# Score matmuls of a decode attention kernel rebuilt as column-tiled units of four octets, with a bf16 score stash and DVE transposes

## The chip, the cores and the metric

The kernel runs on one core of one Trainium2 chip. The metric is the device time of one execution in microseconds (us); the median of several executions is quoted. Engines are named as in the profile: PE is TensorE, DVE is VectorE, ACT is ScalarE, POOL is GpSimd, SP is the engine whose queue issues the loads. PEclk is the clock that the throttle grants to PE, as a share of full speed. PSUM is the on-chip memory into which the kernel lets PE write its results, SBUF the one that holds everything else on the chip. P·V is the product of the attention probabilities and the values. In the tile names, ktp holds K transposes in PSUM, sps scores and ops P·V; arena_k holds the loaded keys and, after the eviction, the transposed ones; arena_v holds the values.

## The reference

One decode step of an adaLN transformer block, one token, bf16. The attention reads a key and a value cache of 65,536 tokens for 8 heads, each shared by 4 query heads: 128 MB of keys and 128 MB of values. Everything else is small.

```python
mod = (silu(c) @ w_mod).reshape(...)                 # six modulation vectors
h = layernorm(x) * (1 + ca) + sa
# attention: Hq = 32, Hkv = 8, Sk = 65536, Dh = 128
q = (h @ wq) ...
scores = einsum('bhqd,bhkd->bhqk', q, k) * Dh ** -0.5   # k, v repeated 4 times
p = softmax(scores)
o = einsum('bhqk,bhkd->bhqd', p, v)
x = x + ga * (o ... @ wo)
h = layernorm(x) * (1 + cb) + sb
return x + gb * ((silu(h @ w_gate) * (h @ w_up)) @ w_down)
```

## The kernel before

Keys and values arrive in 2 MB chunks of 64 token tiles (a tile is 128 tokens), four chunk buffers each. A block of 8 tiles is called an *octet*; a head has 64 octets, a chunk 8. The main loop runs over octets. In step `s` it emits the transposition of octet `s+3` (PE) and its eviction to SBUF (DVE, or ACT for every fourth octet), then the scores of octet `s` (PE). The P·V product of an octet follows 72 octets behind its scores, two octets at a time. A small scheduler adds semaphore waits from declared reads and writes. It never reorders: each engine receives its instructions in the order of emission.

```python
def T_op(o):                     # 4 transposes of 128x128 f32 (pairs of bf16) into one of 3 PSUM banks
    ...
def evac_engine(o):
    if o % 4 == 3 and not in_exp_burst(o): return "act"
    return "dve"

def S_op(o):                     # scores: K is the stationary operand, the queries (M64) stream
    ...
    for pi_ in range(4):
        for par in range(2):
            insts.append(e.matmul(sps[:, sbank, REP*tl : REP*tl + 8*2*REP], lhsT=pair[:, :, par],
                                  rhs=M64[:, g, par, :, :], start=(par == 0), stop=(par == 1)))

def bank_ops(o):                 # once per 8 octets, on DVE: maximum, and a copy to SBUF (f32)
    op("dve", f"bmax{bl}", ...);  op("dve", f"bcopy{bl}", ...)

def head_softmax_ops(g):         # once per head: 8 exps on ACT write P_sb, [token, tile, query head]
    ...
def PVU_op(u):                   # two octets of P*V: 4 column-tiled matmuls
    ...
    for j in range(4):
        lhsT = P_sb[gp][:, tq:tq + 4, :].rearrange("p t h -> p (t h)")
        insts.append(e.matmul(ops_[32*j:32*j + 16, g % 2, 0:512], lhsT=lhsT, rhs=vnat[b][...],
                              start=first, stop=last, tile_position=(0, 32 * j)))
    op("pe", f"PVU{u}", emit, reads=[("vnat", b)] + [("P", gp, pi, h) ...], writes=[("ops", g % 2)])

for s in range(NKO + LV):        # NKO = 512 octets, LV = 72
    o = s + DT                   # DT = 3
    if o < NKO:
        T_op(o); pump_dma(); evac_op(o)
    if s < NKO:
        S_op(s)
        if s % OBL == OBL - 1: bank_ops(s)
        if s % OPH == OPH - 1: pending_heads[s + BC_OFF] = head_of(s)
    if s in pending_heads: head_softmax_ops(pending_heads.pop(s))
    vo = s - LV
    if 0 <= vo < NKO and vo % 2 == 1:
        PVU_op(vo // 2); pump_dma()
```

## Time and profile before

| | before |
|---|---|
| time, median of 16 runs | 696.16 us (695.25 to 698.64) |
| DMA while K and V both stream | 426 GB/s |
| PE / DVE / ACT busy | 79% / 48% / 24% |
| first P·V, last K transposes, end (trace) | 89.6, 624, 694 us |

From the page: the span, the busy us of each engine (share of the span), the rows of the 40 time slices of 17 us for the granted clock and for DMA (each digit in tenths), the GB/s of each slice, and the row of the main load queue (packets, MB, share):

```profile
span 694.0 us, 16865 instructions
...
PE 547.0 (79%) x7781; PEld 451.6 (65%) x7781; DVE 333.5 (48%) x594; ACT 166.9 (24%) x253; POOL 8.8 (1%) x33
...
PEclk9999999998999999999999989999999999996555
DMA  8999999999999999999999999999999999999996
GB/s 332 428 373 371 413 429 426 427 426 426 426 424 429 425 426 426 426 429 426 425 427 428 424 426 427 426 426 426 427 426 426 425 429 424 427 400 395 427 349 239
...
q1 hardware_dynamic: 26472, 285.48, 98.4%
```

DMA is at 9 in almost every slice and moves about 426 GB/s. 285 MB at that rate is 670 us. Clearly below the full rate are the first slice, slices 3 to 5 (only keys are consumed there) and four of the last five. The chain that ended last, by engine and then by line:

```profile
DMA 70%; PE 24%; SPq 4%; DVE 2%; issue 0%; POOL 0%; ACTq 0%; DVEq 0%
DMA arena_k<-in_A_k_cache_dram 39%; DMA arena_v<-in_A_v_cache_dram 24%; PE ktp L449 14%; PE sps L492 6%; SPq L285 4%; DMA xT_bf<-in_A_x_dram 3%; PE ops L559 3%; DMA arena_k<-in_B_w_down_dram 3%; PE misc L574 1%; DVE arena_k L475 1%; PE misc L419 1%; DVE X_sb L568 0%; DVE pm L504 0%; PE misc L675 0%; DVE S_sb L511 0%
```

It is mostly loads of keys and values (SPq is the queue of SP; "issue" is time without a wait that the profile shows). The costliest groups (line, engine, operation, count | busy us, mean ns of one | idle before and who ended it):

```profile
L449 PE MATMUL ktp<-identf,arena_k 128*128 128x128 f32 x2048 | 351.1, 297 | 63.1 <-DMA arena_k<-in_A_k_cache_dram 63.1
L475 DVE COPY arena_k<-ktp 128x512 f32<-128x512 f32 x398 | 274.8, 691 | 258.6 <-PE ktp L449 256.8
...
L492 PE MATMUL sps<-M,arena_k 128*128 128x64 bf16 x4096 | 213.3, 197 | 0.0
...
L559 PE MATMUL ops<-arena_v,P_sb 128*16 128x512 bf16 x1024 | 106.8, 430 | 31.8 <-DMA arena_v<-in_A_v_cache_dram 31.8
```

And a piece of the timeline in the middle (start us, length us, engine, line; lines of other engines left out). It shows P·V, transposes, scores, transposes, scores, P·V following each other on PE without idle time in brackets, that is, without a wait:

```profile
326.26 0.39 PE L559 MATMUL ops<-arena_v,P_sb 128*16 128x512 bf16 x4
...
326.58 0.66 PE L449 MATMUL ktp<-identf,arena_k 128*128 128x128 f32 x4
...
327.08 0.40 PE L492 MATMUL sps<-M,arena_k 128*128 128x64 bf16 x8
...
327.31 0.63 PE L449 MATMUL ktp<-identf,arena_k 128*128 128x128 f32 x4
...
327.78 0.40 PE L492 MATMUL sps<-M,arena_k 128*128 128x64 bf16 x8
...
328.11 0.39 PE L559 MATMUL ops<-arena_v,P_sb 128*16 128x512 bf16 x4
```

### The profile page before, as it was taken

How to read it: one execution, taken by the hardware profiler on the slowest of the kernel's cores; microseconds unless marked ns; L12 is line 12 of the kernel's file. 1: busy time of each engine (PE TensorE's matmuls, PEld its weight loads, DVE VectorE, ACT ScalarE, POOL GpSimd, SP SyncE). 2: the span in 40 equal slices, each digit the busy share in tenths (PEclk: the TensorE clock that was granted, in tenths of full speed). 3: DMA queues.
4: the chain of work that ended last, by engine and by line, in shares of the span. 5: the costliest groups of instructions: out<-in, count | busy, mean ns of one | idle time of the engine just before them, and what ended most of it. 6: DMA issues, size and time to landing. Idle time of an engine off the chain costs nothing.

```text
span 694.0 us, 16865 instructions
## 1 busy us (share of the span) xinstructions
PE 547.0 (79%) x7781; PEld 451.6 (65%) x7781; DVE 333.5 (48%) x594; ACT 166.9 (24%) x253; POOL 8.8 (1%) x33
## 2 busy tenths in 40 slices
PE   1399998888878798887788898878878798785345
PEld 1399987677766686766676686667666676672024
DVE  0178875454545554555454545536544554451001
ACT  0033442232222412123212411214121321223000
POOL 2000000000000000000000000000000000000000
PEclk9999999998999999999999989999999999996555
DMA  8999999999999999999999999999999999999996
GB/s 332 428 373 371 413 429 426 427 426 426 426 424 429 425 426 426 426 429 426 425 427 428 424 426 427 426 426 426 427 426 426 425 429 424 427 400 395 427 349 239
DMA packets 27598, 286.56 MB, mean 413 GB/s; under 512 B 3208, under 2 KB 9096, under 8 KB 10632
## 3 DMA queue, kind: packets, MB, share of 16 engines
q1 hardware_dynamic: 26472, 285.48, 98.4%
q8 instruction: 61, 1.00, 0.6%
q10 hardware_dynamic: 1056, 0.00, 0.1%
q14 instruction: 9, 0.07, 0.0%
HBM read 285.48 MB, written 0.00 MB: 411 GB/s over the span
## 4 chain that ended last, share of the span: by engine, by line
DMA 70%; PE 24%; SPq 4%; DVE 2%; issue 0%; POOL 0%; ACTq 0%; DVEq 0%
DMA arena_k<-in_A_k_cache_dram 39%; DMA arena_v<-in_A_v_cache_dram 24%; PE ktp L449 14%; PE sps L492 6%; SPq L285 4%; DMA xT_bf<-in_A_x_dram 3%; PE ops L559 3%; DMA arena_k<-in_B_w_down_dram 3%; PE misc L574 1%; DVE arena_k L475 1%; PE misc L419 1%; DVE X_sb L568 0%; DVE pm L504 0%; PE misc L675 0%; DVE S_sb L511 0%
## 5 line engine op out<-in xcount | busy, mean ns | idle before, releaser
L449 PE MATMUL ktp<-identf,arena_k 128*128 128x128 f32 x2048 | 351.1, 297 | 63.1 <-DMA arena_k<-in_A_k_cache_dram 63.1
L475 DVE COPY arena_k<-ktp 128x512 f32<-128x512 f32 x398 | 274.8, 691 | 258.6 <-PE ktp L449 256.8
L449 PEld LDWEIGHTS ktp<-identf,arena_k 128*128 128x128 f32 x2048 | 231.1, 148 | 120.2 <-issue 78.6
L477 ACT ACTIVATE arena_k<-ktp 128x1024 bf16<-128x1024 bf16 x114 | 116.7, 1024 | 441.4 <-PE ktp L449 441.4
L492 PE MATMUL sps<-M,arena_k 128*128 128x64 bf16 x4096 | 213.3, 197 | 0.0
L492 PEld LDWEIGHTS sps<-M,arena_k 128*128 128x128 bf16 x4096 | 200.4, 101 | 8.4 <-issue 0.2
L559 PE MATMUL ops<-arena_v,P_sb 128*16 128x512 bf16 x1024 | 106.8, 430 | 31.8 <-DMA arena_v<-in_A_v_cache_dram 31.8
L559 PEld LDWEIGHTS ops<-arena_v,P_sb 128*16 128x16 bf16 x1024 | 24.4, 89 | 56.8 <-DMA arena_v<-in_A_v_cache_dram 41.4
L526 ACT ACTIVATE P_sb<-S_sb,negm 128x64 bf16<-128x64 f32 (+1 forms) x64 | 47.1, 858 | 0.3
L504 DVE TENSOR_REDUCE pm<-sps 128x4 f32<-128x256 f32 x64 | 26.6, 416 | 2.0 <-PE sps L492 2.0
L511 DVE COPY S_sb<-sps 128x256 f32<-128x256 f32 x64 | 26.5, 414 | 0.0
L568 DVE COPY X_sb<-ops 128x512 f32<-128x512 f32 x8 | 5.5, 682 | 36.9 <-PE ops L559 36.9
L574 PE MATMUL misc<-sel,X_sb 128*128 128x4 f32 x64 | 10.1, 281 | 10.9 <-DVE X_sb L568 10.9
L574 PEld LDWEIGHTS misc<-sel,X_sb 128*128 128x128 f32 x64 | 9.6, 229 | 13.9 <-issue 7.2
L526 ACT ACTIVATION_READ_ACCUMULATOR P_sb<-S_sb,negm 128x1 f32 x64 | 14.2, 222 | 0.0
L379 PE MATMUL misc<-sT,arena_v 128*128 128x1 bf16 x96 | 2.7, 165 | 14.2 <-DVE sT L371 14.2
L661 ACT ACTIVATE g_e<-g_c 128x14 f32<-128x14 f32 x1 | 0.2, 214 | 54.9 <-DVE g_c L659 54.9
L379 PEld LDWEIGHTS misc<-sT,arena_v 128*128 128x128 bf16 x96 | 2.6, 104 | 14.2 <-issue 14.2
L509 POOL CROSS_LANE_REDUCE rmax<-pmax 128x4 f32<-128x4 f32 x8 | 3.9, 484 | 594.4 <-PE sps L492 384.0
L636 PE MATMUL misc<-attnT,arena_k 128*128 128x1 bf16 x128 | 3.6, 165 | 6.0 <-DMA arena_k<-in_A_wo_dram 6.0
L392 PE MATMUL misc<-xT,mmat 128*128 128x4 f32 x2 | 0.6, 350 | 8.8 <-DVE modT L383 8.8
L636 PEld LDWEIGHTS misc<-attnT,arena_k 128*128 128x128 bf16 x128 | 3.5, 104 | 6.2 <-DMA arena_k<-in_A_wo_dram 6.2
(85 smaller groups left out, 47.9 us busy)
## 6 DMA issues: line engine op xcount, KB each, us to landing
arena_k<-in_A_k_cache_dram SPq DMA_DIRECT2D x64, 2048.0 KB, 31.2
arena_v<-in_A_v_cache_dram SPq DMA_DIRECT2D x64, 2048.0 KB, 30.6
arena_v<-in_A_wq_dram SPq DMA_DIRECT2D x1, 4096.0 KB, 22.2
arena_k<-in_A_wo_dram SPq DMA_DIRECT2D x1, 4096.0 KB, 28.8
arena_v<-in_w_mod_dram SPq DMA_DIRECT2D x1, 3072.0 KB, 11.3
arena_k<-in_B_w_gate_dram SPq DMA_DIRECT2D x1, 1792.0 KB, 32.9
arena_k<-in_B_w_up_dram SPq DMA_DIRECT2D x1, 1792.0 KB, 14.6
arena_k<-in_B_w_down_dram SPq DMA_DIRECT2D x1, 1792.0 KB, 17.9
```

The costliest lines, as they stand in the source:

```text
L285: return [e.dma_start(out_ap, in_ap)]
L419: insts.append(e.matmul(misc[:, 64 + hd:64 + hd + 1], lhsT=wq_sb[:, kt, hd * P:(hd + 1) * P], rhs=hT[:, kt:kt + 1], start=(kt == 0), stop= ...
L449: insts.append(e.transpose(ktp[:, bank, pi_ * P:(pi_ + 1) * P], knat32[b][:, j * 4 + pi_, :], identf[:, :]))
L475: emit = lambda e: [e.tensor_copy(ring32[r], ktp[:, bank, :])]
L477: emit = lambda e: [e.activation(out=ring[r], in_=ktp[:, bank, :].bitcast(BF16), func=ACT.Copy)]
L492: insts.append(e.matmul(sps[:, sbank, REP * tl:REP * tl + 8 * 2 * REP], lhsT=pair[:, :, par], rhs=M64[:, g, par, :, :], start=(par == 0), ...
L504: op("dve", f"bmax{bl}", lambda e: [e.tensor_reduce(out=pm4[:, :, k], in_=hview, axis=AX.X, op=ALU.max)], reads=[("sps", sbank)], writes=[ ...
L511: op("dve", f"bcopy{bl}", lambda e: [e.tensor_copy(S_sb[gp][:, :, k * BLT:(k + 1) * BLT], hview)], reads=[("sps", sbank)], writes=[("S", g ...
L526: return [e.activation(out=P_sb[gp][:, t0:t1, h], in_=S_sb[gp][:, h, t0:t1], func=ACT.Exp, bias=negm[gp][:, h:h + 1], scale=SCALE, accum_o ...
L559: insts.append(e.matmul(ops_[32 * j:32 * j + 16, g % 2, 0:512], lhsT=lhsT, rhs=vnat[b][:, tl0 + 4 * j:tl0 + 4 * j + 4, :], start=first, st ...
L574: insts.append(e.matmul(misc[:, 8:8 + REP], lhsT=X_sb[:, tau * P:(tau + 1) * P], rhs=sel[:, tau, :], start=(tau == 0), stop=(tau == 3)))
L636: insts.append(e.matmul(misc[:, 96 + jb:96 + jb + 1], lhsT=wo_sb[:, kt, jb * P:(jb + 1) * P], rhs=attnT[:, kt:kt + 1], start=(kt == 0), st ...
```

## The change

Intent: PE loads 4,096 score weights of 128x128 for little work. The change swaps the operands: the queries, 8 columns, are stationary in four column tiles of the array, and the keys stream 512 wide. A *unit* of four octets then needs 8 matmuls instead of 32. The scores land with the query heads on partitions, 32 tokens wide per block. So the softmax has one exp over bf16 for all heads at once (copied out of PSUM by ACT into a stash), and the probabilities are brought back to tokens on partitions by a DVE transpose of 32x32 blocks and a compaction, just before each P·V group.

```diff
+        def SU_op(u):                                   # replaces S_op and bank_ops, once per 4 octets
+                for par in range(2):
+                    for a in range(4):
+                        insts.append(e.matmul(sps[32 * a:32 * a + 2 * REP, sbank, 0:512], lhsT=M8[:, g, par, :],
+                                              rhs=R4[:, :, 32 * a:32 * a + 32, par],
+                                              start=(par == 0), stop=(par == 1), tile_position=(0, 32 * a)))
+            op("dve", f"smax{u}", lambda e: [e.tensor_reduce(out=pmu[...], in_=sps[:, sbank, :], axis=AX.X, op=ALU.max)], ...)
+            op("act", f"scopy{u}", lambda e: [e.activation(out=S_st[gp][...], in_=sps[:, sbank, :], func=ACT.Copy)], ...)
 ...
         def PVU_op(u):
+            op("dve", f"ptr{u}", lambda e: [e.transpose(out=PTraw[wb][:, :], in_=S_st[gp][:, wh * 256:(wh + 1) * 256])], ...)
+            op("dve", f"pcp{u}", lambda e: [e.tensor_copy(PT[gp][...], PTraw[wb][...][:, :, 0:2 * REP])], ...)
-                    lhsT = P_sb[gp][:, tq:tq + 4, :].rearrange("p t h -> p (t h)")
+                    lhsT = PT[gp][:, tq * REP:(tq + 4) * REP]
-               reads=[("vnat", b)] + [("P", gp, pi, h) for pi in pis for h in range(REP)],
+            op("pe", f"PVU{u}", emit, reads=[("vnat", b), ("PT", gp, wh)], writes=[("ops", g % 2)])
 ...
-                S_op(s)
-                if s % OBL == OBL - 1:
-                    bank_ops(s)
+                if s % SU == SU - 1:
+                    SU_op(s // SU)
```

Cut: buffers, masks that pick a head's rows for the maximum and the sums, the exps.

More of the change, by code (lines that the diff above doesn't have):

```diff
@@ L144, in bass_adaLN_cond__gqa_block_cached__swiglu_ffn__decode_kernel @@
     CPH = TPH // TPC
-    BLT = min(64, TPH)
-    WN = 16
-    assert REP * BLT + 8 * 2 * REP <= 512
-    OBL = BLT // 8
-    NBL = TPH // BLT
+    SU = 4
+    assert OPH % SU == 0
+    UPH4 = OPH // SU
     NKO = HKV * OPH
@@ L155, in bass_adaLN_cond__gqa_block_cached__swiglu_ffn__decode_kernel @@
     RT = 8
+    assert RT % SU == 0
     NB = 3
@@ L162, in bass_adaLN_cond__gqa_block_cached__swiglu_ffn__decode_kernel @@
     EPS = 1e-5
-    if TPH > TPC:
-        PIECES = [(0, TPC), (TPC, TPH)]
+    U0 = max(1, OPC // SU)
+    if UPH4 > U0:
+        PIECES = [(0, U0), (U0, UPH4)]
     else:
-        PIECES = [(0, TPH)]
+        PIECES = [(0, UPH4)]
     NPIECE = len(PIECES)
@@ L205, in bass_adaLN_cond__gqa_block_cached__swiglu_ffn__decode_kernel @@
         wq_sb = arena_v[:, 2 * CH_ELEMS: 2 * CH_ELEMS + wq_elems].rearrange("p (kt n) -> p kt n", n=HQD)
-        S_sb = [sb(f"S_sb{i}", [P, REP, TPH], FP32) for i in range(2)]
-        P_sb = [sb(f"P_sb{i}", [P, TPH, REP], BF16) for i in range(2)]
+        S_st = [sb(f"S_st{i}", [P, UPH4 * 512], BF16) for i in range(2)]
+        PT = [sb(f"PT{i}", [P, TPH * REP], BF16) for i in range(2)]
+        PTraw = [sb(f"PTraw{i}", [P, 256], BF16) for i in range(2)]
         ident = sb("ident", [P, P], BF16)
@@ L214, in bass_adaLN_cond__gqa_block_cached__swiglu_ffn__decode_kernel @@
         M8 = sb("M8", [P, HKV, 2, 2 * REP], BF16)
-        M64 = sb("M64", [P, HKV, 2, 8, 2 * REP], BF16)
         mmat = sb("mmat", [P, P], FP32)
@@ L234, in bass_adaLN_cond__gqa_block_cached__swiglu_ffn__decode_kernel @@
         qT = sb("qT", [P, HQ], BF16)
-        pm4 = sb("pm4", [P, REP, NBL], FP32)
-        pmax = sb("pmax", [P, REP], FP32)
+        pmu = sb("pmu", [P, UPH4], FP32)
+        pmax_p = sb("pmax_p", [P, 1], FP32)
+        pm4 = sb("pm4", [P, REP], FP32)
+        onehot = sb("onehot", [P, REP], FP32)
+        maskneg = sb("maskneg", [P, REP], FP32)
+        negt = sb("negt", [P, REP], FP32)
         rmax = sb("rmax", [1, REP], FP32)
-        negm = [sb(f"negm{i}", [P, REP], FP32) for i in range(2)]
-        lpart = sb("lpart", [P, HQ, NPIECE], FP32)
-        lsum = sb("lsum", [P, HQ], FP32)
+        negm_p = [sb(f"negm_p{i}", [P, 1], FP32) for i in range(2)]
+        lpart = sb("lpart", [P, HKV, NPIECE], FP32)
+        lsum_all = sb("lsum_all", [P, HKV], FP32)
+        lsum = sb("lsum", [P, HKV, REP], FP32)
         rl = sb("rl", [P, HQ], FP32)
@@ L319, in bass_adaLN_cond__gqa_block_cached__swiglu_ffn__decode_kernel @@
             op("dve", f"opsz{i}", lambda e, i=i: [e.memset(ops_[:, i, :], 0.0)], writes=[("ops", i)])
+            op("dve", f"spsz{i}", lambda e, i=i: [e.memset(sps[:, i, :], 0.0)], writes=[("sps", i)])
+        op("pool", "oh0", lambda e: [e.memset(onehot[:, :], 0.0)], writes=[("onehot",)])
+        for a in range(4):
+            for tau in range(2):
+                op("pool", f"oh{a}{tau}", lambda e, a=a, tau=tau: [e.affine_select(out=onehot[:, :], in_=onehot[:, :], pattern=[[-1, REP]],
+                                                                                 compare_op=ALU.not_equal, fill=1.0,
+                                                                                 base=-(32 * a + 4 * tau), channel_multiplier=1)],
+                   reads=[("onehot",)], writes=[("onehot",)])
+        op("dve", "maskneg", lambda e: [e.tensor_scalar(out=maskneg[:, :], in0=onehot[:, :], scalar1=-1.0, scalar2=1e30, op0=ALU.add, op1=ALU.mult)],
+           reads=[("onehot",)], writes=[("maskneg",)])
         x_col = A_x.rearrange("a b (j p) -> p (a b j)", p=P)
@@ L433, in bass_adaLN_cond__gqa_block_cached__swiglu_ffn__decode_kernel @@
         op("dve", "M8d", lambda e: [e.tensor_copy(M8[H2:P, :, 1, REP:2 * REP], qa_v(H2, P))], reads=[("misc",)], writes=[("M8",)])
-        for par in range(2):
-            op("dve", f"M64_{par}", lambda e, par=par: [e.tensor_copy(M64[:, :, par, :, :],
-                                                                      M8[:, :, par, :].unsqueeze(2).broadcast_to([P, HKV, 8, 2 * REP]))],
-               reads=[("M8",)], writes=[("M64", par)])
         pump_dma()
@@ L478, in evac_op, with piece_of_unit @@
             op(eng, f"E{o}", emit, reads=[("ktp", bank)], writes=[("ring", r)])
-        def S_op(o):
-            g = head_of(o)
-            r = o % RT
-            bl = o // OBL
-            sbank = bl % 2
-            th0 = (o % OPH) * 8
+        def piece_of_unit(uh):
+            for pi, (u0, u1) in enumerate(PIECES):
+                if u0 <= uh < u1:
+                    return pi
+            raise AssertionError
+        def SU_op(u):
+            o0 = SU * u
+            g = head_of(o0)
+            gp = g % 2
+            uh = u % UPH4
+            sbank = u % 2
+            r0 = o0 % RT
+            R4 = arena_k[:, ring_base + r0 * 8 * P: ring_base + (r0 + SU) * 8 * P].rearrange(
+                "p (sp q two) -> p sp q two", q=P, two=2)
@@ L486, in emit @@
             def emit(e):
                 insts = []
-                for pi_ in range(4):
-                    tl = (th0 + 2 * pi_) % BLT
-                    pair = ring[r][:, pi_ * 2 * P:(pi_ + 1) * 2 * P].rearrange("p (s two) -> p s two", two=2)
-                    for par in range(2):
-                        insts.append(e.matmul(sps[:, sbank, REP * tl:REP * tl + 8 * 2 * REP], lhsT=pair[:, :, par],
-                                              rhs=M64[:, g, par, :, :], start=(par == 0), stop=(par == 1)))
@@ L494, in emit @@
-                return insts
-            op("pe", f"S{o}", emit, reads=[("ring", r), ("M64", 0), ("M64", 1)], writes=[("sps", sbank)])
-        def bank_ops(o):
-            g = head_of(o)
-            gp = g % 2
-            bl = o // OBL
-            k = bl % NBL
-            sbank = bl % 2
-            hview = sps[:, sbank, 0:REP * BLT].rearrange("p (t h) -> p h t", h=REP)
-            op("dve", f"bmax{bl}", lambda e: [e.tensor_reduce(out=pm4[:, :, k], in_=hview, axis=AX.X, op=ALU.max)],
-               reads=[("sps", sbank)], writes=[("pm4", k)])
-            if k == NBL - 1:
-                op("dve", f"pmax{g}", lambda e: [e.tensor_reduce(out=pmax[:, :], in_=pm4[:, :, :], axis=AX.X, op=ALU.max)],
-                   reads=[("pm4", kk) for kk in range(NBL)], writes=[("pmax",)])
-                op("pool", f"rmax{g}", lambda e: [e.tensor_reduce(out=rmax[0:1, :], in_=pmax[:, :], axis=AX.C, op=ALU.max)],
-                   reads=[("pmax",)], writes=[("rmax",)])
-            op("dve", f"bcopy{bl}", lambda e: [e.tensor_copy(S_sb[gp][:, :, k * BLT:(k + 1) * BLT], hview)],
-               reads=[("sps", sbank)], writes=[("S", gp, k)])
+                for par in range(2):
+                    for a in range(4):
+                        insts.append(e.matmul(sps[32 * a:32 * a + 2 * REP, sbank, 0:512], lhsT=M8[:, g, par, :],
+                                              rhs=R4[:, :, 32 * a:32 * a + 32, par],
+                                              start=(par == 0), stop=(par == 1), tile_position=(0, 32 * a)))
@@ new lines, in emit @@
+                return insts
+            op("pe", f"SU{u}", emit, reads=[("ring", (r0 + i) % RT) for i in range(SU)] + [("M8",)], writes=[("sps", sbank)])
+            op("dve", f"smax{u}", lambda e: [e.tensor_reduce(out=pmu[:, uh:uh + 1], in_=sps[:, sbank, :], axis=AX.X, op=ALU.max)],
+               reads=[("sps", sbank)], writes=[("pmu", uh)])
+            op("act", f"scopy{u}", lambda e: [e.activation(out=S_st[gp][:, uh * 512:(uh + 1) * 512], in_=sps[:, sbank, :], func=ACT.Copy)],
+               reads=[("sps", sbank)], writes=[("S", gp, uh)])
@@ new lines, in SU_op @@
+            if uh == UPH4 - 1:
+                op("dve", f"pmaxp{g}", lambda e: [e.tensor_reduce(out=pmax_p[:, :], in_=pmu[:, :], axis=AX.X, op=ALU.max)],
+                   reads=[("pmu", i) for i in range(UPH4)], writes=[("pmax_p",)])
+                op("dve", f"pm4_{g}", lambda e: [e.scalar_tensor_tensor(out=pm4[:, :], in0=onehot[:, :], scalar=pmax_p[:, 0:1], in1=maskneg[:, :],
+                                                                       op0=ALU.mult, op1=ALU.add)],
+                   reads=[("pmax_p",), ("onehot",), ("maskneg",)], writes=[("pm4",)])
+                op("pool", f"rmax{g}", lambda e: [e.tensor_reduce(out=rmax[0:1, :], in_=pm4[:, :], axis=AX.C, op=ALU.max)],
+                   reads=[("pm4",)], writes=[("rmax",)])
@@ L517, in head_softmax_ops, with emit @@
                reads=[("ones",), ("rmax",), ("misc",)])
-            op("act", f"negm{g}", lambda e: [e.activation(out=negm[gp][:, :], in_=misc[:, 0:REP], func=ACT.Copy, scale=-SCALE)],
-               reads=[("misc",)], writes=[("negm", gp)])
-            for pi, (t0, t1) in enumerate(PIECES):
-                ks = sorted(set(t // BLT for t in range(t0, t1)))
-                for h in range(REP):
-                    col = g * REP + h
-                    def emit(e, h=h, t0=t0, t1=t1, col=col, pi=pi):
-                        return [e.activation(out=P_sb[gp][:, t0:t1, h], in_=S_sb[gp][:, h, t0:t1], func=ACT.Exp,
-                                             bias=negm[gp][:, h:h + 1], scale=SCALE,
-                                             accum_out=lpart[:, col, pi:pi + 1])]
-                    op("act", f"exp{g}_{pi}_{h}", emit,
-                       reads=[("negm", gp)] + [("S", gp, kk) for kk in ks],
-                       writes=[("P", gp, pi, h), ("lpart", col, pi)])
-        def piece_of(th):
-            for pi, (t0, t1) in enumerate(PIECES):
-                if t0 <= th < t1:
-                    return pi
-            raise AssertionError
+            op("dve", f"negt{g}", lambda e: [e.scalar_tensor_tensor(out=negt[:, :], in0=misc[:, 0:REP], scalar=-SCALE, in1=onehot[:, :],
+                                                                    op0=ALU.mult, op1=ALU.mult)],
+               reads=[("misc",), ("onehot",)], writes=[("negt",)])
+            op("dve", f"negp{g}", lambda e: [e.tensor_reduce(out=negm_p[gp][:, :], in_=negt[:, :], axis=AX.X, op=ALU.add)],
+               reads=[("negt",)], writes=[("negm_p", gp)])
+            for pi, (u0, u1) in enumerate(PIECES):
+                def emit(e, u0=u0, u1=u1, pi=pi):
+                    reg = S_st[gp][:, u0 * 512:u1 * 512]
+                    return [e.activation(out=reg, in_=reg, func=ACT.Exp, bias=negm_p[gp][:, 0:1], scale=SCALE,
+                                         accum_out=lpart[:, g, pi:pi + 1])]
+                op("act", f"exp{g}_{pi}", emit,
+                   reads=[("negm_p", gp)] + [("S", gp, uu) for uu in range(u0, u1)],
+                   writes=[("S", gp, uu) for uu in range(u0, u1)] + [("Pst", gp, pi), ("lpart", g, pi)])
         UPH = OPH // 2
@@ L549, in PVU_op @@
             tl0 = jo * 8
-            pis = sorted(set(piece_of(th0 + i) for i in range(16)))
-            first = (u % UPH == 0)
-            last = (u % UPH == UPH - 1)
+            wh = u % UPH
+            wb = u % 2
+            first = (wh == 0)
+            last = (wh == UPH - 1)
+            su_h = wh // 2
+            pi_ = piece_of_unit(su_h)
+            op("dve", f"ptr{u}", lambda e: [e.transpose(out=PTraw[wb][:, :], in_=S_st[gp][:, wh * 256:(wh + 1) * 256])],
+               reads=[("Pst", gp, pi_), ("S", gp, su_h)], writes=[("PTraw", wb)])
+            op("dve", f"pcp{u}", lambda e: [e.tensor_copy(PT[gp][:, wh * 64:(wh + 1) * 64].rearrange("p (b i) -> p b i", i=2 * REP),
+                                                         PTraw[wb][:, :].rearrange("p (b i) -> p b i", i=32)[:, :, 0:2 * REP])],
+               reads=[("PTraw", wb)], writes=[("PT", gp, wh)])
             def emit(e):
@@ L562, in emit @@
                 return insts
-            op("pe", f"PVU{u}", emit,
-               reads=[("vnat", b)] + [("P", gp, pi, h) for pi in pis for h in range(REP)],
-               writes=[("ops", g % 2)])
+            op("pe", f"PVU{u}", emit, reads=[("vnat", b), ("PT", gp, wh)], writes=[("ops", g % 2)])
             pv_done_octets[0] = vo0 + 2
@@ L622, in bass_adaLN_cond__gqa_block_cached__swiglu_ffn__decode_kernel @@
             epilogue_loads()
-        op("dve", "lsum", lambda e: [e.tensor_reduce(out=lsum[:, :], in_=lpart[:, :, :], axis=AX.X, op=ALU.add)],
-           reads=[("lpart", col, pi) for col in range(HQ) for pi in range(NPIECE)], writes=[("lsum",)])
-        op("pe", "mm_ltot", lambda e: [e.matmul(misc[:, 0:HQ], lhsT=ones_f[:, :], rhs=lsum[:, :], start=True, stop=True)],
+        op("dve", "lsum_all", lambda e: [e.tensor_reduce(out=lsum_all[:, :], in_=lpart[:, :, :], axis=AX.X, op=ALU.add)],
+           reads=[("lpart", g, pi) for g in range(HKV) for pi in range(NPIECE)], writes=[("lsum_all",)])
+        op("dve", "lsum", lambda e: [e.tensor_tensor(out=lsum[:, :, :], in0=lsum_all[:, :].unsqueeze(2).broadcast_to([P, HKV, REP]),
+                                                     in1=onehot[:, :].unsqueeze(1).broadcast_to([P, HKV, REP]), op=ALU.mult)],
+           reads=[("lsum_all",), ("onehot",)], writes=[("lsum",)])
+        op("pe", "mm_ltot", lambda e: [e.matmul(misc[:, 0:HQ], lhsT=ones_f[:, :], rhs=lsum[:, :, :].rearrange("p g h -> p (g h)"), start=True, stop=True)],
            reads=[("ones",), ("lsum",), ("misc",)])
```

## The prediction

> **What bounds the kernel now.** DMA. The slice table shows DMA at 9 tenths almost everywhere and 424 to 429 GB/s from about 90 us to 600 us; the queue table has the K/V queue at 98.4%. 285 MB at 426 GB/s is 670 of the 694 us. PE (79%), DVE (48%) and ACT (24%) hide under it. Only about 22 us are not at full rate: the first load, the K-only stage (35 to 80 us, 373 GB/s, where PE paces each block of 8 token tiles, an "octet", at 0.70 us in the timeline), and the last 60 us. Freeing PE can win some 3% at most.
>
> **Removed.** Per octet 8 score matmuls (0.23 us); per 8 octets two DVE instructions (0.42 us each).
>
> **Added.** Per 4 octets ("unit"): 8 column-tiled 512-wide matmuls (estimate 0.55 us, from the 0.33 us that the existing group of 4 for P·V takes), a 512-wide maximum on DVE out of PSUM (estimate 0.68 us, like the 691 ns eviction of that size), a copy on ACT (about 0.6 us). Per 2 octets two DVE instructions: a 128x256 bf16 transpose, estimated at 0.40 us (the Trainium skill, "VectorE: DVE Perf Modes", The three transpose paths, gives 311 ns for 128x128; no run here shows one yet), and a 0.15 us compaction. DVE sums to about 500 us: occupancy fits.
>
> **Why I expect slower.** Not busy time but order. Each P·V group on PE now waits for its own transpose and compaction. Those stand in DVE's queue behind the eviction of the octet that PE transposed just before and, every second time, the new maximum. The next K transposes stand behind the blocked P·V. So per 2 octets PE and DVE run in series. Chain from the trace's durations at full clock:
> - pair without maximum: P·V 0.33, two K transposes to their end 1.10, eviction 0.69, transpose and compaction 0.6, handovers 0.2: 2.9 us;
> - pair with it: P·V and first K transpose 1.0, two evictions 1.35, maximum 0.68, transpose and compaction 0.6, handovers: 3.7 us.
>
> That is 6.6 us a unit, where DMA needs 4.9. About 109 units lie between the first P·V and the last K transpose.
>
> PE is then busy only some 53% of the time. Before, the granted clock fell to 0.50 for 3.5 to 4 us after most windows 45 to 60% busy (the Trainium skill, "TensorE: Matmul & The Clock Gate", Part 1, describes such a gate with a window of about 3.4 us; the trace agrees with its length). At half clock K transposes take 0.91 us each instead of 0.47, and the unit about 8.9 us. I expect it cold about half of the time: some 7.5 us a unit.
>
> **Sum.** 86 us to the first P·V (its K-only stage is now DVE-paced at about 0.69 us an octet: no gain), 109 x 7.5 = 818, 15 for P·V sums at head ends, 58 from the last K to the end: about 960 us with the mixed clock, 880 at full clock, 1,100 all cold. I predict 950 us, range 840 to 1,060. Chances: faster 0.02, same 0.04, slower 0.94.
>
> **What would show it.** DMA near 300 GB/s in the middle slices; P·V matmuls waiting for the compaction, among the largest waits of PE; the chain of waits mostly PE and DVE instead of DMA; score matmuls' busy time well under 213 us; clock often 0.5; the DVE transpose near 0.40 us.
>
> **What would make it wrong.** If the P·V groups do not wait (DVE ahead of PE), DMA still binds and the time is 690 to 698. If the clock stays full, about 860; a much dearer DVE transpose or a cold clock throughout, over 1,050.

## The result, and the profile after

| | before | after |
|---|---|---|
| time, median | 696.16 us (16 runs) | 1,076.04 us (11 runs, 1,065.83 to 1,079.26) |
| ratio | | 1.5438 (95%: 1.5407 to 1.547) |
| first P·V | 89.6 us | 104.4 us |
| last K transpose ends | 624 us | 1,005 us |
| end | 694 us | 1,075.4 us |

Ratios are the mean time of one kernel's runs over that of the other's of the same rounds, so not quite the ratio of the quoted medians. The change is 54% slower, outside the range (840 to 1,060).

The same parts of the page, after:

```profile
span 1075.4 us, 11287 instructions
...
PE 690.3 (64%) x4709; PEld 405.3 (38%) x4709; DVE 517.6 (48%) x1132; ACT 252.1 (23%) x277; POOL 10.4 (1%) x42
...
PEclk9999666656666566665666556665666665666665
DMA  9879977656766577675766657676676775753698
GB/s 366 344 286 431 415 258 284 244 225 248 275 259 261 208 266 278 246 272 199 277 260 256 259 206 282 249 254 259 219 285 246 264 272 204 266 185 128 234 392 283
...
q1 hardware_dynamic: 26472, 285.48, 70.3%
```

DMA moves about 250 GB/s in the middle and is mostly below 80% busy. No compute engine is full either: PE 64%, DVE 48%. The granted clock is at 6 tenths nearly throughout. The chain by engine and by line:

```profile
PE 59%; DVE 29%; DMA 4%; ACT 3%; issue 3%; SPq 2%; POOL 0%; ACTq 0%; DVEq 0%
PE ktp L459 35%; PE ops L574 11%; PE sps L510 10%; DVE arena_k L485 8%; DVE pmu L515 8%; DVE PTraw L563 8%; DVE PT L565 4%; SPq L290 2%; DMA xT_bf<-in_A_x_dram 2%; DMA arena_k<-in_B_w_down_dram 2%; ACT arena_k L487 1%; PE misc L587 1%; ACT S_st L517 1%; ACT S_st L540 1%; DVE X_sb L581 0%
```

The chain has moved from loads to PE and DVE. The groups:

```profile
L485 DVE COPY arena_k<-ktp 128x512 f32<-128x512 f32 x398 | 273.2, 691 | 430.7 <-PE ktp L459 429.9
L459 PE MATMUL ktp<-identf,arena_k 128*128 128x128 f32 x2048 | 421.1, 372 | 14.2 <-ACT arena_k L487 14.1
...
L574 PE MATMUL ops<-arena_v,PT 128*16 128x512 bf16 x1024 | 137.1, 538 | 320.3 <-DVE PT L565 307.3
...
L510 PE MATMUL sps<-arena_k,M 128*8 128x512 bf16 x1024 | 122.5, 572 | 0.8 <-ACT arena_k L487 0.8
L563 DVE STREAM_TRANSPOSE PTraw<-S_st 128x256 bf16<-128x256 bf16 x256 | 111.3, 435 | 0.1
...
L565 DVE COPY PT<-PTraw 128x64 bf16<-128x64 bf16 x256 | 46.9, 183 | 8.9
```

PE is idle 320 us in front of P·V (line 574), nearly always until DVE's compaction (`DVE PT L565`) is done, and DVE is idle 430 us in front of the evictions, until PE's transposes are done. The list of waits (who waited for whom: total us, times, longest) says the same:

```profile
DVE arena_k L485 <- PE ktp L459: 429.9, 365, 2.6
...
PE ops L574 <- DVE PT L565: 307.3, 227, 2.0
```

Two engines that wait for each other in turn: the timeline of one unit, at half clock. Weight loads and ACT are left out, and the second half is cut to the P·V that ends it; brackets give the idle time before and its releaser.

```profile
598.99 0.60 PE L574 MATMUL ops<-arena_v,PT 128*16 128x512 bf16 x4 [1.35 <-DVE PT L565]
...
599.52 1.97 PE L459 MATMUL ktp<-identf,arena_k 128*128 128x128 f32 x8
600.68 0.69 DVE L485 COPY arena_k<-ktp 128x512 f32<-128x512 f32 x1 [1.74 <-PE ktp L459]
...
601.42 1.02 PE L510 MATMUL sps<-arena_k,M 128*8 128x512 bf16 x8
601.53 0.69 DVE L485 COPY arena_k<-ktp 128x512 f32<-128x512 f32 x1 [0.16 <-PE ktp L459]
602.50 0.69 DVE L515 TENSOR_REDUCE pmu<-sps 128x1 f32<-128x512 f32 x1 [0.28 <-PE sps L510]
603.11 0.43 DVE L563 STREAM_TRANSPOSE PTraw<-S_st 128x256 bf16<-128x256 bf16 x1
...
603.58 0.18 DVE L565 COPY PT<-PTraw 128x64 bf16<-128x64 bf16 x1
...
603.82 0.60 PE L574 MATMUL ops<-arena_v,PT 128*16 128x512 bf16 x4 [1.37 <-DVE PT L565]
...
607.67 0.60 PE L574 MATMUL ops<-arena_v,PT 128*16 128x512 bf16 x4 [1.35 <-DVE PT L565]
```

Read it from top to bottom. P·V (598.99) runs, then the K transposes of two octets (599.52), two evictions on DVE (600.68, 601.53), the maximum (602.50), which at half clock also waits for the score matmuls (601.42), the transpose (603.11), the compaction (603.58), and only then the next P·V (603.82). What overlaps is only the first eviction with the second octet's transposes, and the second with the scores. From P·V to P·V this takes 4.83 us, the other half of the unit 3.85 us: 8.68 us a unit.

### The profile page after: what moved, and what is told of

It reads as the page before. It is cut to its first block, busy times and chain, and to the rows that moved or that the text cites. A ratio compares the mean times of both kernels' runs of the same rounds, so it can differ in the third digit from the quotient of the medians.

```text
span 1075.4 us, 11287 instructions
## 1 busy us (share of the span) xinstructions
PE 690.3 (64%) x4709; PEld 405.3 (38%) x4709; DVE 517.6 (48%) x1132; ACT 252.1 (23%) x277; POOL 10.4 (1%) x42
## 3 DMA queue, kind: packets, MB, share of 16 engines
q1 hardware_dynamic: 26472, 285.48, 70.3%
## 4 chain that ended last, share of the span: by engine, by line
PE 59%; DVE 29%; DMA 4%; ACT 3%; issue 3%; SPq 2%; POOL 0%; ACTq 0%; DVEq 0%
PE ktp L459 35%; PE ops L574 11%; PE sps L510 10%; DVE arena_k L485 8%; DVE pmu L515 8%; DVE PTraw L563 8%; DVE PT L565 4%; SPq L290 2%; DMA xT_bf<-in_A_x_dram 2%; DMA arena_k<-in_B_w_down_dram 2%; ACT arena_k L487 1%; PE misc L587 1%; ACT S_st L517 1%; ACT S_st L540 1%; DVE X_sb L581 0%
## 5 line engine op out<-in xcount | busy, mean ns | idle before, releaser
L459 PE MATMUL ktp<-identf,arena_k 128*128 128x128 f32 x2048 | 421.1, 372 | 14.2 <-ACT arena_k L487 14.1
L459 PEld LDWEIGHTS ktp<-identf,arena_k 128*128 128x128 f32 x2048 | 334.0, 193 | 105.8 <-issue 87.2
L574 PE MATMUL ops<-arena_v,PT 128*16 128x512 bf16 x1024 | 137.1, 538 | 320.3 <-DVE PT L565 307.3
L517 ACT ACTIVATE S_st<-sps 128x512 bf16<-128x512 f32 x128 | 76.2, 596 | 578.4 <-DVE pmu L515 578.4
L574 PEld LDWEIGHTS ops<-arena_v,PT 128*16 128x16 bf16 x1024 | 25.6, 89 | 466.4 <-DVE PT L565 416.5
L510 PE MATMUL sps<-arena_k,M 128*8 128x512 bf16 x1024 | 122.5, 572 | 0.8 <-ACT arena_k L487 0.8
L563 DVE STREAM_TRANSPOSE PTraw<-S_st 128x256 bf16<-128x256 bf16 x256 | 111.3, 435 | 0.1
L515 DVE TENSOR_REDUCE pmu<-sps 128x1 f32<-128x512 f32 x128 | 88.3, 690 | 32.1 <-PE sps L510 32.1
L540 ACT ACTIVATE S_st<-S_st,negm_p 128x1024 bf16<-128x1024 bf16 (+1 forms) x16 | 59.2, 3702 | 25.0 <-DVE negm_p L535 25.0
L565 DVE COPY PT<-PTraw 128x64 bf16<-128x64 bf16 x256 | 46.9, 183 | 8.9
```

The costliest lines, as they stand in the source:

```text
L459: insts.append(e.transpose(ktp[:, bank, pi_ * P:(pi_ + 1) * P], knat32[b][:, j * 4 + pi_, :], identf[:, :]))
L510: insts.append(e.matmul(sps[32 * a:32 * a + 2 * REP, sbank, 0:512], lhsT=M8[:, g, par, :], rhs=R4[:, :, 32 * a:32 * a + 32, par], start=(p ...
L515: op("dve", f"smax{u}", lambda e: [e.tensor_reduce(out=pmu[:, uh:uh + 1], in_=sps[:, sbank, :], axis=AX.X, op=ALU.max)], reads=[("sps", sb ...
L517: op("act", f"scopy{u}", lambda e: [e.activation(out=S_st[gp][:, uh * 512:(uh + 1) * 512], in_=sps[:, sbank, :], func=ACT.Copy)], reads=[( ...
L540: return [e.activation(out=reg, in_=reg, func=ACT.Exp, bias=negm_p[gp][:, 0:1], scale=SCALE, accum_out=lpart[:, g, pi:pi + 1])]
L563: op("dve", f"ptr{u}", lambda e: [e.transpose(out=PTraw[wb][:, :], in_=S_st[gp][:, wh * 256:(wh + 1) * 256])], reads=[("Pst", gp, pi_), (" ...
```

## The experiments

Theory: PE's P·V group waits for a transpose that stands late in DVE's queue, and this series, stretched by the clock that PE loses when it idles, is the whole loss. Rivals: the added work costs the time by its amount; the tiled matmuls lower the clock by themselves. Eight kernels ran, in two calls. Each was timed beside the kernel before on the same chip (696.42 us in the first call, 696.48 us in the second).

### 1. The transposes one place earlier in DVE's queue

```diff
         for s in range(NKO + LV):
+            po = s - LV                      # same step, but before its eviction and maximum
+            if 0 <= po < NKO and po % 2 == 1:
+                PT_op(po // 2)               # ptr and pcp, taken out of PVU_op
             o = s + DT
```

> The same instructions as the changed kernel; only the transpose and compaction of a P·V group are issued at the start of the step, before that step's eviction and maximum, so one place earlier in DVE's queue. Order theory (P·V waits behind the eviction and maximum of the octet just transposed): the wait of P·V for the compaction falls from 307 us to under 100 us, a unit of 4 octets takes about 4.9 us (DMA) in the middle, total 700 to 740 us. Work theory (the added DVE, ACT and PE instructions themselves cost the time): 1040 to 1080 us, as the work is unchanged. Clock theory (the column-tiled matmuls make the clock fall by themselves): the clock stays near 0.62 and the total above 850 us.

Measured: 701.77 us, ratio 1.0074 (1.0054 to 1.0094). The instructions are the same in number and kind as in the changed kernel. The wait of P·V in the list of waits, and the rates in the 40 slices:

```profile
PE ops L581 <- DVE PT L557: 59.2, 154, 1.8
```

```profile
GB/s 330 427 304 318 321 429 427 429 423 430 428 425 428 425 428 426 427 428 428 426 427 426 430 424 427 430 423 430 424 428 430 426 425 427 428 427 405 426 354 231
```

The wait fell from 307 to 59 us, and the middle runs at DMA's rate again. DVE is busy 489.5 us here (70% of the shorter span; 517.6 us in the changed kernel), so its occupancy was no obstacle. The work theory falls. So does the rival about the clock: with the same tiled matmuls the granted clock of the run is 0.909.

### 2. The transposes four octets earlier

```diff
+        PT_LEAD = 4
+            po = s - LV + PT_LEAD
```

> Transpose and compaction are issued four steps (four octets) before their P·V group. Order theory: P·V never waits for the compaction (under 20 us in all), the middle runs at DMA's 425 GB/s; the K-only stage is still as slow as in the changed kernel (first P·V near 104 us against 85 before), so 705 to 720 us, ratio to before about 1.02. Work theory: 1040 to 1080 us.

Measured: 701.29 us, ratio 1.0066 (1.005 to 1.0083); P·V waits 15 us for the compaction in all. That is below the forecast of 705 to 720 us. A longer lead wins nothing over the first experiment, since DMA already binds. The first P·V is at 102.3 us (89.6 us before), so the key-only stage is still slow.

### 3. The same place, but P·V waits for nothing on DVE

Its output is wrong, which doesn't matter for the time. Every DVE instruction stays where the change put it, but P·V reads a constant tile.

```diff
-                    lhsT = PT[gp][:, tq * REP:(tq + 4) * REP]
+                    lhsT = cst[:, :]
-            op("pe", f"PVU{u}", emit, reads=[("vnat", b), ("PT", gp, wh)], writes=[("ops", g % 2)])
+            op("pe", f"PVU{u}", emit, reads=[("vnat", b), ("cst",)], writes=[("ops", g % 2)])
```

> Result wrong on purpose. The changed kernel with every instruction in its old place, DVE's transposes and compactions included; only the P·V groups read a constant tile as weights instead of the compacted probabilities, so they wait for nothing on DVE. If it is PE's wait that costs the time: 698 to 712 us, DMA at 425 GB/s in the middle. If the place or the amount of the DVE work costs it whether or not PE waits: over 1000 us.

Measured: 700.37 us, ratio 1.0055 (1.0036 to 1.0073). So late DVE work does no harm by itself; the wait of PE for it does. One more thing follows: the comparison with the reference passed this kernel although its attention weights are constants. The attention's share of the output is too small here for the comparison to notice, so a pass in this case says little about the attention path.

### 4. Filling PE's waits, to measure the clock's share

Ten matmuls, 256 wide, with unused results, stand in front of each P·V group up to the last K transposes, where PE would idle. Order and waits stay.

```diff
+            if vo0 + 1 + LV + DT < NKO:
+                op("pe", f"dum{u}", lambda e: [e.matmul(ops_[:, (g + 1) % 2, 0:256], lhsT=dum[:, 0:P], rhs=dum[:, 0:256],
+                                                        start=True, stop=True) for _ in range(10)], ...)
             op("pe", f"PVU{u}", emit, ...)
```

> The changed kernel plus 10 idle-time matmuls (256 wide, into an unused PSUM bank, result unused) in front of each P·V group; they should fit into its 1.35 us wait at full clock. If the serial order sets the number of steps and the low clock only stretches each: clock in the middle over 0.95, a unit 6.5 to 6.8 us, total 890 to 930 us. If the clock is not what I mis-sized, or these matmuls do not lift it: 1076 us or more.

Measured: 880.32 us, ratio 1.2638 (1.2612 to 1.2663), 10 us below the forecast of 890 to 930. More work on PE makes the kernel 196 us faster. The stage between the first P·V and the last K transpose, first of the changed kernel, then of this one (window us, length; busy us of each engine; the three last columns are granted clock, DMA share, GB/s):

```profile
core 0: us, PE busy (x) PEld busy (x) DVE busy (x) ACT busy (x) POOL busy (x), PEclk, DMA share, GB/s
105.00:1000.00 895.00, 591.26 (x3517) 340.09 (x3516) 431.15 (x912) 208.37 (x232) 2.90 (x6) 0.62 0.67 252
```

```profile
105.00:805.00 700.00, 619.83 (x5649) 423.15 (x5647) 407.93 (x908) 206.22 (x228) 2.90 (x6) 1.00 0.86 320
```

At full clock the first P·V is at 102.0 us and the last K transposes start at 809.6 us: 708 us for 109 units and 7 head ends, 6.5 us a unit with the head ends (the median unit, by the starts of the P·V groups, is 6.30 us). So the loss of 380 us divides into about 196 us for the low clock and 184 us for the series at full clock, the slower key-only stage included.

### 5. Fewer fillers

```diff
-  for _ in range(10)
+  for _ in range(4)
```

> As the warmed kernel, with 4 filling matmuls per P·V group instead of 10: PE is then busy about 66% of a unit at full clock and about 87% at half clock. If the clock follows PE's busy share with a limit near 60%: mostly warm, 890 to 960 us, clock in the middle 0.8 or more. If a fixed amount of matmul work or the mere absence of gaps decides, it stays near 1076 us.

Measured: 885.96 us, ratio 1.2719 (1.269 to 1.2748), a little faster than the forecast. The same stage:

```profile
105.00:805.00 700.00, 484.69 (x4316) 300.45 (x4316) 404.65 (x900) 204.63 (x226) 2.90 (x6) 0.98 0.84 319
```

PE is busy 69% of this stage at a clock of 0.98. In the changed kernel it is busy 66% at 0.62. So the busy share over the whole stage does not tell the two apart. The share window by window does: the clock records in these traces are 1.0 or 0.5 and nothing else, and they change at multiples of 3.41 us. In this stage of the changed kernel, each of the 61 stretches at full clock lasted one such window, with PE 36 to 52% busy. Of the 61 stretches at half clock, 27 lasted one window (92 to 98% busy), 26 lasted four (13.7 us, about 69% busy, more in the last window) and 7 lasted 24 to 41 us.

The same stage in all ten traces (from about the first P·V to the last K transposes), cut into these windows, agrees. PE busy is as the profile counts it, K transposes included, and eight of the ten kernels have no fillers. Of 238 full-clock windows less than 50% busy, 231 were followed by half clock; of 1,035 busier ones, 25. Of 277 half-clock windows less than 80% busy, none was followed by full clock; of 287 busier ones, 255. With four fillers there are only four low stretches in 700 us; they lasted two to four windows although PE was 82 to 93% busy in them, so the share is not a sure rule.

### 6. The slow key-only stage: ACT's copy behind its eviction

Before the first P·V, a unit of the changed kernel takes 3.58 us. Its timeline in that stage (only the lines of the chain):

```profile
51.54 0.60 PE L510 MATMUL sps<-arena_k,M 128*8 128x512 bf16 x8
...
52.25 0.68 DVE L515 TENSOR_REDUCE pmu<-sps 128x1 f32<-128x512 f32 x1
52.97 0.60 ACT L517 ACTIVATE S_st<-sps 128x512 bf16<-128x512 f32 x1 [2.07 <-DVE pmu L515]
...
53.46 1.02 ACT L487 ACTIVATE arena_k<-ktp 128x1024 bf16<-128x1024 bf16 x1
...
54.53 0.66 PE L459 MATMUL ktp<-identf,arena_k 128*128 128x128 f32 x4 [0.93 <-ACT arena_k L487]
```

PE's next K transposes (54.53) wait for a PSUM bank that ACT evicts (53.46). ACT evicts late, because its queue holds the score copy (52.97) in front, and that waits for DVE's maximum (52.25): the kernel's own scheduler lets readers of one PSUM tile follow each other only in order. The edit issues the copy one step later:

```diff
-            op("act", f"scopy{u}", ...)              # in SU_op
+            if 1 <= s <= NKO and s % SU == 0:
+                SC_op(s // SU - 1)                    # the same copy, after the next step's eviction
```

> The changed kernel with the ACT copy of a score unit issued one step later, behind ACT's eviction instead of in front of it. Theory for the slow K-only stage (PE's third PSUM bank waits for ACT's eviction, which stands behind the copy, which waits for the DVE maximum): a unit there falls from 3.58 us to 2.7 to 3.0 us, first P·V from 104 to 88 to 94 us, the rest unchanged, total 1060 to 1068 us. If DVE's own work paces that stage: no change.

Measured: 1,064.33 us, ratio 1.5279 (1.5249 to 1.531). The first P·V is at 91.6 us, and a unit takes 2.90 us. The same place in its timeline:

```profile
54.20 1.02 ACT L487 ACTIVATE arena_k<-ktp 128x1024 bf16<-128x1024 bf16 x1 [1.38 <-PE ktp L459]
...
55.12 0.59 ACT L530 ACTIVATE S_st<-sps 128x512 bf16<-128x512 f32 x1
...
55.27 0.66 PE L459 MATMUL ktp<-identf,arena_k 128*128 128x128 f32 x4 [0.24 <-ACT arena_k L487]
```

ACT evicts first (54.20) and copies after that (55.12); PE's wait falls from 0.93 to 0.24 us.

### 7. Both repairs together

> Transposes issued four steps early and ACT's score copy issued one step later, both together. The two repairs act on different stages, so they should add: first P·V near 90 us instead of 102, middle at DMA's rate. The K-only stage then delivers about 360 to 380 GB/s, like before. Total 693 to 698 us, ratio to before 0.995 to 1.003. If the slow K-only stage costs nothing in the end (DMA catching up later), it stays at 701 us.

The edit is that of experiments 2 and 6 together. Measured: 692.42 us, ratio 0.9938 (0.9925 to 0.995). That is just below the forecast of 693 to 698 us. The repairs add up to within 3 us, and this version is 0.6% faster than the kernel before. The first P·V is at 89.1 us and the last K transposes start at 618.1 us, with DMA at 427 GB/s between.

### 8. ACT takes more evictions

```diff
-            if o % 4 == 3 and not in_exp_burst(o):
+            if (o % 4 == 3 or o % 8 == 1) and not in_exp_burst(o):
```

> The kernel above, and ACT takes three of eight evictions instead of two of eight outside the softmax bursts. In the K-only stage DVE's share per unit falls from 2.70 us to about 2.35 us, below the 2.46 us that DMA needs, so that stage should run at 410 GB/s or more: total 688 to 693 us, ratio 0.989 to 0.996, a little faster than before. If ACT's order makes new waits there: 696 us or more.

Measured: 692.36 us, ratio 0.9939 (0.9925 to 0.9952): no gain over experiment 7. The total lies in the forecast, but the reason given for it is a miss: slices 3 and 4 of the page, in the key-only stage, run at 375 and 372 GB/s, not at 410 or more, although DVE is now busy 459 us instead of 490. The unit of the key-only stage is still 2.90 us (in the timeline K transposes of three octets start at 51.02, 53.92 and 56.81 us), with PE still waiting 0.24 us for ACT in each:

```profile
51.72 1.02 ACT L487 ACTIVATE arena_k<-ktp 128x1024 bf16<-128x1024 bf16 x1 [1.38 <-PE ktp L459]
...
52.80 0.66 PE L459 MATMUL ktp<-identf,arena_k 128*128 128x128 f32 x4 [0.24 <-ACT arena_k L487]
```

DVE's share of the evictions was not what paces that stage. What remains there is PE's own 2.66 us and the 0.24 us that it waits for ACT's eviction, which takes 1.02 us.

## Why the prediction was right or wrong

The direction and the mechanism were right; the size was wrong, by 125 us in the trace. The prediction's sum against it:

| term | predicted us | measured us |
|---|---|---|
| up to the first P·V | 86 | 104.4 |
| 109 units and the head ends | 818 + 15 | 900.7 |
| after the last K transpose | 58 | 70.3 |
| sum | 977, given as 960, then as 950 | 1,075.4 |

- **DMA bound before, at most 3% to win: right.** With the waits removed, the rebuilt kernel reaches 692.42 us, DMA at 427 GB/s.
- **"Not busy time but order": right, and shown** by three kernels: the same instructions one place earlier (701.77 us), four octets earlier (701.29 us), or P·V without the dependence (700.37 us). The Trainium skill, "TensorE: Matmul & The Clock Gate", Part 2, says that matmuls stay in program order; the trace agrees: in the unit shown, the K transposes emitted behind P·V begin 0.53 us after it, and the profile names no wait of their own for them.
- **The unit's length: right, within 5%.** Predicted 6.6 us at full clock, measured 6.30 us with fillers (6.5 us with the head ends); predicted 8.9 us at half clock, measured 8.68 us. That the prediction's 880 us for full clock is what the filled kernel took (880.32 us) is partly luck: its stages took 102, 708 and 69 us where the prediction's terms are 86, 734 (109 x 6.6 + 15) and 58, and the errors cancel.
- **"I expect it cold about half of the time": the step that failed.** The clock of the stage was 0.62; as it is granted at 1.0 or 0.5, that is 76% of the time at half clock ((1 - 0.62) / 0.5). The unit was 8.26 us (900 us over 109, head ends included), not 7.5. This term alone is 68 us short. The prediction gives no reason for the half, and its own remarks pointed to more: it put PE at some 53% busy and had seen the clock fall after most windows 45 to 60% busy. What it left out is the return. At full clock every window was 36 to 52% busy and the clock fell after each; at half clock PE was mostly about 69% busy, and no window under 80% brought full clock back (experiment 5). With 76% in place of half of the time, the prediction's own 6.6 and 8.9 us give 8.2 us a unit, by estimate.
- **"Its K-only stage is now DVE-paced at about 0.69 us an octet: no gain": wrong**, 18 us. It was 0.895 us (3.58 us for four), paced by the chain over DVE's maximum and ACT's copy to ACT's eviction, as experiment 6 shows: without it the first P·V moves from 104.4 to 91.6 us. Some 4 us of the 18 were a misreading of before, whose first P·V is at 89.6 us and not at 86 us (nor at the 85 us in the expectation of experiment 2).
- **58 us after the last K: 12 us short, and wrong for before too.** The kernel before already takes 70 us there (624 to 694 us), the changed one 70.3 and the filled one 69.3, so the change added next to nothing to this stage.
- **The sum was not carried through.** The terms add to 977 us, the text says 960 and predicts 950: 27 us lost by rounding down. The text's own figure for a clock that is low throughout is 1,100 us; the stated range of 840 to 1,060 left it out.
- **The smaller marks:** score matmuls busy 122.5 us (well under 213: right); the DVE transpose of 128x256 435 ns (0.40 us predicted), 124 ns more than the 311 ns that the Trainium skill, "VectorE: DVE Perf Modes", The three transpose paths, gives for 128x128, a size that no run here shows; compaction 183 ns (150 predicted); DMA 252 GB/s in the middle (near 300 predicted).

## What to carry to other kernels

Busy times that fit are not enough: when a new instruction on one in-order engine feeds another in-order engine, look at what stands in front of it in its queue, and whether that waits for the engine it feeds. If so, issue it earlier; here one place was worth 374 us. An idle PE was charged twice here, once for the wait (184 us with the key-only stage) and once for the clock (196 us). So estimate the clock from two busy shares, the one at full speed and the one at half speed: in these traces the clock nearly always held when the first was above 50%, and never came back while the second was under 80%.

## What the Trainium skill lacked or had wrong

- "TensorE: Matmul & The Clock Gate", Part 1 and "Why this matters for your kernels": it warns of idle gaps longer than about 3 us. Here no gap of PE between the first P·V and the last K transposes was longer than 2.0 us, and the clock was still halved 76% of the time. Part 1 also tells of a kernel whose short idles between groups of matmuls made the clock oscillate, which is closer, but it gives no busy share. Here 231 of 238 full-clock windows under 50% busy were followed by half clock, and 25 of 1,035 busier ones.
- The same page says that one busy window of about 3.4 us brings full clock back, but not how busy it must be. Here none of 277 windows under 80% busy did, and 255 of 287 busier ones.
- No page describes two in-order engines that wait for each other in turn. Here it showed as PE 64% busy, DVE 48% and the K/V queue at 70.3%.
